# ScalarE as a further way for the weights' top halves into their bank and for the exponents' shift, in a new order of the work

## The chip, the cores and the metric

The kernel runs on one core of a Trainium2 chip. The metric is the device time of one execution in microseconds (us). A core has a matrix engine (TensorE, PE in the profile; PEld is its loading of the stationary operand), three engines for elementwise work (VectorE or DVE, ScalarE or ACT, GpSimd or POOL), and a queue that issues its transfers (SyncE or SP). Each engine works through its own list of instructions in order and waits where an operand is not there yet.

## What is computed

Attention over the 32 largest scores of each row, then two dense blocks over the 2304 tokens that come out of it:

```python
# q, k, v: 4 batches x 8 heads x 576 tokens x 64
scores = (q @ k.T) / 8
kth    = 32nd largest of each row
attn   = softmax(where(scores >= kth, scores, -1e9))
x = (attn @ v) rearranged to 2304 tokens x 512
h = x @ w_in                                   # 512 x 2048
x = (h * sigmoid(1.702 * h)) @ w_out           # 2048 x 512
a, b = x @ w1, x @ w2                          # 512 x 1024 each
out = (a * b @ w3) @ w4                        # 1024 x 1024, 1024 x 512
```

All inputs are float32. The kernel keeps more than one half-width number's precision by splitting each operand of a product into a high and a low float16 part and taking three products (high times high, low times high, high times low).

## The kernel before

The 2304 tokens are 18 tiles of 128 rows, and each tile has 8 heads, so there are 144 heads in order. For one head (`head`), TensorE makes the scores `S` (L1119, 128 x 576, in a bank pair `s_ps`), VectorE finds the 32 largest of each row by four rounds of eight (`max` L1139, with `match_replace` L1142 between them), and ScalarE makes the cut (L1157: entries under the 32nd largest are pushed far away; this frees the score bank) and the exp (L1160). The exp reads its shift, called `nb`, from one column: (32nd largest minus largest) times the head's scale. It is made by one one-column instruction (L1149) on GpSimd or on VectorE. The exp's result is split into a high part (L1172, or L1226 on GpSimd) and a low part (L1175, L1178), turned by a DMA (L1181), and multiplied with V on TensorE (L1195, L1197). When a tile has all its heads, `moe` runs the two dense blocks for it, whose products are the 512-column matmuls of L769 to L771.

The weights come in during the first 200 us, in 72 blocks of 128 x 512 (`load64`). They are stored as 64-bit words, so a block arrives as 512 KB (L487, on SyncE's queue), and four steps make a float32 of it: its upper bits are copied as a float16 ("top", L499 on ScalarE, L502 on GpSimd or L505 on VectorE); these are put into a PSUM bank ("pass", `f_pass`, L508: a matmul with the identity); VectorE shifts the lower word and ORs it with the bank ("join", L513), which frees the raw block's buffer for the next load. Six raw buffers and two more pairs hold arriving blocks. After the join come the weights' scaling and their split (`l2_scale`, with the squares on TensorE in L551; `split`: L599 or L605 high part, L608/L611 on TensorE or L621 on ScalarE, or L627/L624/L628 on GpSimd for the rest), the transposes of w3 (L680, L683) and the product of w3 and w4 (L806).

The work's order is not the order of the code. Every step is an `op` with one or more alternatives (engine, cost, function). A table `PLAN` holds a rank and the number of the chosen alternative for each step; `Order.run` sorts the steps by rank and issues them, each on the engine chosen, taking buffers from the pools in that order. What an engine does next is therefore fixed in the table, and a step that is late holds up everything behind it on its engine. The names in the profile are those of memory areas: `wout`, `win`, `w` and `usb` are stores that several kinds of data pass through, so `wout<-w` in L499 may be a block of any weight.

Of the kernel before, what the change touches and what calls it, by code (L numbers as in the profile page):

```python
# [37 lines left out]
class Order:  # L38
# [120 lines left out]
    'Tx+Yf)7ooYweH$LZLl^{yP^HndTFz?x!MwKmv%rqs2$QyYEQJMnxO-|f?h+ft=H3=>n-$_dON+dzF$9}U(}(2b!?2%=4t!23)&oQq4rSobU!^^K#zdM+A8gr'
    'hV-S{IxR?#(sSws0y+dZy3}*&dG!0*BdwTTU9YP*3TPI1O?#jX*Qe`;wNu&-{kZ-}e;m*=aG!ojzplT~JL!G&5Bg`_Gtvac27c6k=xL42Mt^;jp4&(?iW$j?'  # L160
    'jS|C*Tt*F}p|Mimq7OGF7>kV~fky+U==1f>#ulT8F~~S;+%z5-4+EouYwEQEQuVg_25qx;M!Tf#)h_yLx~^x^{R4va?0P;UDX^MR%V?!{)Til7^jZ3xfTj9!'
    '{i8<ow0e5Isoqr|pbyfQ>8teB`eyx(epi2>KhuBdzx7OpztLNtr(f2u=-c$2`YwI1eo{Xba6!MVS2x-kV~r_BPraW$SRbMf)ko-)^_luyeWAWvKh*GG!_y5{'
    'BwS6nmT)s+t-d~CUBZTh1qo*p4kw&T=wfs?dKrC<0mcYpv@zb8XiPQc8uJp@C2maoXXNr_@D=b)H)b}P(P%-VO~$swt%-XR^BM(>!bTCJs8P}=Ym_s}8+DBe'
    'M*YN&iTxAn8SNW2Xw;!mYonC!MPQ1rj?pqPHL+{r5@V^c%vf%$GIkjIj6=p5<FcX5Kr_OOH18*7Gz~Me`6w}yFTF3DFO6Bmm(EwxM-1EW8KFicqjF$Pqlxid'
    '|EIe~Izt%&fq_PdabJI_ztMl{aYnq6$0%XE)8FfVb#Cl24jRXe6GmsFPvA6Tj#0&^8raHcXN)u^8>@}A#$n@>amBc93^axsD~vV91><7iGvl*S+h}TxF=iQ8'
    'joZd2!!&OhcZ}!8E915C&iG<{HGUX>{~r?Fv`k<^Q<|<BVEW7uGt|s$#+$Xwie^J|t~oz-Uh0C>>}FM8PG1XOp`_wTm6EC_)k$ib+9q{yYGE@eH956r>S}Xc'
    '(%PgANnOlg=0tOnS=$_t+9Y*gYE)7QGtMky)-Zef>ihcm5|hfC70hbp5Ob_=q;IjWvf0^J&)418${gdH<6GrxpETUp)i=UNOxyHKKXbS7Eii`}YdWUCub`P='
    'zBkgEdCYv~G;^!D&D?LcHjnx)nm5fV=2UaKxyw9lUNxVXFU@o2H#5BzY*|(&E5r)5u9@$BepUtxT3M_}E6OTl^|A(8L#<*~D{HJZ&RT74ur^tntpnB}>x%Wj'
    'YGkIGjm>6ebF;rW${cS_HfNX{%}q%GL0N->f)*v6_nq?H@jXv^;d|@*?ptFXPdbuxE9s~C+x%<(GfgY4mCnj&`K)j&+R9^<Y@FD*RO13x#h`?sN<lfT;z7BB'
    '$_5p+QiJLRH4VyV<+lo2MXd5xW2?E<*6L_=wz^vVtzp&(Yn0W;8g31-##r;MMa32uTT*PfwX)cXVrz=svF=*;t%uet>z(!4`f2^P{#gV_;0Jsl9ApNSL2XbU'  # L170
    '<OX>`MNkFg1bIMFkN|XGf%G5%#DG{(5MVQl8E%#Y$sh$Z2W>%j&;twx<G?uMn(@*2X>cD1DjZZUsJc~JucJ5Co9J!yF#%%(o(EL3rdrdjh1M=>NbvaJ3BhMU'
    'IWvb9Yb9AFti3@ef=&h%hb3SQSQCzfsUgim+J<z8&){dMA%Zwc6Ph+OHnc131_!~(a0;9eGACq3$XS>jRYWyWEmQ~94sB7gL&;CjhYF%Xs5B}SRywRqSVKGt'
    'twUST4zwrqeCXAZk4pBy>+w#!4`0Eb!hVPS35y|(a9=zH&%m?8=7cQ>+Yla0^U>n81f4@WMs$kkAF+TEJI2ms7qH7kmW-?v*)B2<ZAaVF`Sc528nHfNL&ROm'
    '?RdMh-POKs_lz76IWO|FEm$gR&W1&8iMkQ>HtHW6Wv{Zg+S~0zk-H+#M_!8D%WrZ+xFVxS8yy&3E_%1f$J_DYd;~woM`mvp-63X^*e8yPW8%2D6n!W9LG&-N'
# [1391 lines left out]
```

## Time and profile before

| | us |
|---|---|
| median of 3 runs | 959.38 (959.14 to 960.53) |
| the profiled execution's own time | 956.57 |
| its span, first to last instruction | 954.8 |
| TensorE busy | 929.9 (97%) |
| VectorE busy | 870.4 (91%) |
| GpSimd busy | 781.8 (82%) |
| ScalarE busy | 676.4 (71%) |

The time lies 1.8 us above the span in the profiled execution, and that execution lies 2.8 us under the median. The program has three parts: in the first 50 us the weights and the first queries and keys arrive, and no engine is full; to 206 us heads 4 to 24 and the weights' work share all engines; from there on the weights are done and heads and dense blocks alternate. Matmuls overlap in TensorE's pipeline, so the recorded length of one (0.38 us) is longer than the distance to the next (0.216 us for 512 columns); the busy times of the table are unions and count the overlap once.

### The profile page before, as it was taken

The page shows a single profiled execution, that of the slowest core. Times are in us where ns is not written, and L with a number is a line of the kernel's source. Part 1 is how long each engine was busy: PE and PEld are TensorE (multiplying, and loading weights), DVE is VectorE, ACT ScalarE, POOL GpSimd, SP SyncE. Part 2 cuts the span into 40 slices and gives each one's busy share as a digit, 9 for nine tenths or more (in the row PEclk, how much of TensorE's full clock was granted, in tenths as well). Part 3 has the DMA queues.
Part 4 walks back from the last instruction along what each step waited for, and adds up shares of the span by engine and source line. Part 5 has one row for each costly group of instructions (what it writes and reads, how often), then busy time and mean ns, then how long its engine had stood idle before and what let it go on. Part 6 is the DMA issues. An engine that isn't in the chain of part 4 may idle for free.

```text
span 954.8 us, 19723 instructions
## 1 busy us (share of the span) xinstructions
PE 929.9 (97%) x6685; PEld 489.0 (51%) x6688; DVE 870.4 (91%) x1870; ACT 676.4 (71%) x1221; POOL 781.8 (82%) x1071
## 2 busy tenths in 40 slices
...
GB/s 302 309 293 324 283 256 204 204 121 128 161 155 145 163 154 130 146 127 154 147 162 115 171 122 139 146 150 156 128 132 131 117 123 138 127 83 116 55 3 34
DMA packets 397861, 149.30 MB, mean 156 GB/s; under 512 B 375872, under 2 KB 384064, under 8 KB 397760
## 3 DMA queue, kind: packets, MB, share of 16 engines
...
## 4 chain that ended last, share of the span: by engine, by line
PE 88%; DMA 5%; DVE 2%; POOL 1%; issue 1%; SPq 1%; ACT 1%; DVEq 0%; POOLq 0%; ACTq 0%
PE mm L769 23%; PE mm L770 22%; PE mm L771 22%; PE s_ps L1119 7%; PE mm L1197 4%; PE mm L806 3%; PE mm L1195 2%; DMA w<-in_moe_w_in_dram 1%; PE mm L551 1%; DMA w<-in_moe_w_dram 1%; DMA usb<-usb 1%; PE mm L611 1%; DVE ysb L1142 1%; DMA ats<-ysb 1%; PE mm L508 1%
## 5 line engine op out<-in xcount | busy, mean ns | idle before, releaser
L1139 DVE MAX8 m8s<-ysb 128x8 f32<-128x576 f32 x432 | 321.9, 755 | 6.1
L1142 DVE MATCH_REPLACE8 ysb<-m8s,ysb 128x576 f32<-128x576 f32 x288 | 214.0, 744 | 0.0
L1178 POOL TENSOR_TENSOR ysb<-ysb 128x512 f16<-128x512 f32 x144 | 167.9, 1169 | 0.3
L1157 ACT ACTIVATE ysb<-s_ps,m8s 128x576 f32<-128x576 f32 x144 | 106.5, 739 | 68.2 <-DVE m8s L1139 57.0
L1160 ACT ACTIVATE ysb<-ysb,nbs,small 128x576 f32<-128x576 f32 x144 | 123.9, 864 | 8.3 <-POOL nbs L1149 5.7
L771 PEld LDWEIGHTS <-usb 128*128 128x128 f16 x804 | 78.6, 98 | 95.0
L769 PE MATMUL mm<-w,usb 128*128 128x512 f16 x329 | 124.8, 379 | 2.2 <-DMA usb<-usb 1.6
L771 PE MATMUL mm<-w,usb 128*128 128x512 f16 x329 | 124.7, 379 | 0.0
L770 PE MATMUL mm<-w,usb 128*128 128x512 f16 x329 | 124.7, 379 | 0.0
L769 PEld LDWEIGHTS <-usb 128*128 128x128 f16 x804 | 78.5, 98 | 85.8 <-issue 2.7
L770 PEld LDWEIGHTS <-usb 128*128 128x128 f16 x804 | 78.6, 98 | 80.1 <-issue 0.9
L1139 DVE MAX8 m8s<-s_ps 128x8 f32<-128x576 f32 x144 | 108.7, 755 | 2.6 <-PE s_ps L1119 1.7
L1142 DVE MATCH_REPLACE8 ysb<-m8s,s_ps 128x576 f32<-128x576 f32 x144 | 107.9, 749 | 0.0
L1119 PE MATMUL s_ps<-kts,qts 128*128 128x288 f16 (+1 forms) x640 | 95.9, 290 | 1.3 <-ACT ysb L1157 1.3
L769 PE MATMUL mm<-wout,usb 128*128 128x512 f16 x239 | 90.6, 379 | 0.0
L771 PE MATMUL mm<-wout,usb 128*128 128x512 f16 x239 | 90.6, 379 | 0.0
L770 PE MATMUL mm<-wout,usb 128*128 128x512 f16 x239 | 90.6, 379 | 0.0
L769 PE MATMUL mm<-win,usb 128*128 128x512 f16 x236 | 89.4, 379 | 0.0
L771 PE MATMUL mm<-win,usb 128*128 128x512 f16 x236 | 89.4, 379 | 0.0
L770 PE MATMUL mm<-win,usb 128*128 128x512 f16 x236 | 89.4, 379 | 0.0
L1317 POOL TENSOR_TENSOR usb<-usb 128x512 f16<-128x512 f32 x59 | 68.4, 1161 | 16.1 <-issue 7.8
L1119 PEld LDWEIGHTS <-qts 128*128 128x128 f16 (+1 forms) x640 | 55.8, 101 | 41.0 <-issue 10.2
...
## 6 DMA issues: line engine op xcount, KB each, us to landing
...
```

What stands on the lines that cost most here:

```text
L769: nc.tensor.matmul(o, a[:, i, :], hi, start=(first and i == 0), stop=False)
L770: nc.tensor.matmul(o, a[:, i, :], lo, start=False, stop=False)
L771: nc.tensor.matmul(o, a[:, 4 + i, :], hi, start=False, stop=(last and i == 3))
L806: nc.tensor.matmul(E["mm"], e["f"][:, n * P : (n + 1) * P], E4[4 * kc + n]["w"], start=kc == 0 and n == 0, stop=kc == 1 and n == 3,)
L1119: nc.tensor.matmul(E["sp"][r : r + n, i], qe[q_][:, h, r : r + n], kt[:, j * S + i * HS : j * S + (i + 1) * HS], start=k_ == 0, stop=k_ == 1,)
L1139: nc.vector.max(out=E["m8"][:, 8 * i : 8 * i + 8], in_=E["sp"] if i == 0 else E["w"])
L1142: nc.vector.match_replace(out=two(E["w"]) if i == 0 else E["w"], in_to_replace=E["m8"][:, 8 * i : 8 * i + 8], in_values=E["sp"] if i == 0 ...
L1157: nc.scalar.activation(two(E["y"]), E["sp"], AF.Prelu, bias=E["m8"][:, TOPK - 1 : TOPK], scale=-1.0, alpha=1.0 / FAR)
L1160: nc.scalar.activation(E["y"], E["y"], AF.Exp, bias=E["nb"], scale=nesc)
L1178: return lambda: eng.tensor_tensor(hl()[:, S + SR : 2 * S], *y_of(at_main, SM), op=ALU.subtract)
L1197: nc.tensor.matmul(o[:, 0 : D + 1], at_, v2[:, j_, blk, D : P + 1], start=i == 0, stop=i == 8)
L1317: return lambda: eng.tensor_tensor(E["h"][:, C : 2 * C], src(), E["h"][:, 0:C], op=ALU.subtract)
```

## The change

It does three things.

1. `load64` gets a second way for the pass: a ScalarE copy of the top halves into the PSUM bank, beside the matmul with the identity.
2. `head` gets a third way for the shift: a pair of one-column ScalarE instructions. The first gives the 32nd largest minus the largest (Prelu with slope 1, scale -1 and a column as bias), the second multiplies it with the head's scale.
3. `PLAN` is another table: other ranks, and other alternatives chosen, among the old ones too.

```diff
+        def f_pass_a():
+            nc.scalar.copy(E["mm"], E["w"].bitcast(BF16)[:, 0:C])
+
...
-        ps_ = pe(0.22, due, f_pass, deps=[tp], env=E, acq=["mm"], tag="w pass")
+        ps_ = op([("T", 0.22, f_pass, 0.0), ("A", 0.5, f_pass_a, 0.0)], due, deps=[tp], env=E, acq=["mm"], tag="w pass")
...
+        def f_nb_a():
+            nc.scalar.activation(E["nb"], E["m8"][:, 0:1], AF.Prelu, bias=E["m8"][:, TOPK - 1 : TOPK], scale=-1.0, alpha=1.0)
+            nc.scalar.activation(E["nb"], E["nb"], AF.Copy, scale=esc)
+
...
-            [("G", 0.35, f_nb(nc.gpsimd), 0.0), ("V", 0.178, f_nb(nc.vector), NB_DVE)], due - 6, deps=[d, X["esc", hp]],
+            [("G", 0.35, f_nb(nc.gpsimd), 0.0), ("V", 0.178, f_nb(nc.vector), NB_DVE), ("A", 0.22, f_nb_a, 0.0)], due - 6, deps=[d, X["esc", hp]],
...
 PLAN = (
-    'c-jru1A87z00rRHaA#&`c2g_K7bi`cq;`_pO=`EPZQHhO+qP}nwt4S=IOja?(KJIdHK-BI)jTbW=BFiSNm`<2X+Xmo)3_$J^jZcjn--}B_=jtOnoo<?Vzgxc'
...
+    'c-jq@17jUa07h3cv!mUa-J18tO`4?Xt=%SRn<i~kyGd=^wr$(CZQHiZ_x{6&a}-5YG(}ga;wYJwoQj{Pgc7ZkRG@+sQ^5*TEKdec7LUIY;0abjl`y4{Qc6iw'
```

In the changed program the pass is a matmul for 25 of the 72 blocks and a ScalarE copy for 47 (at L511; lines after it stand 3 further down, and those after the new shift 7). The shift is on ScalarE for 94 heads (L1159 and L1160 there), on GpSimd for 36 instead of 101, and on VectorE for 14 instead of 43 (a tile that lies across two batches has more than one instruction). ScalarE has 12 fewer scalings of weights (32 to 27 of L599, 12 to 5 of L621) and 18 fewer high parts of the exp (110 to 92), GpSimd 18 more of these. The number of transfers is the same.

The first place is TensorE between the scores of head 5 and the next ones, where w3 and w4 are multiplied. Before, three passes stand there:

```order
L1119 MATMUL s_ps_89<-kts,qts 128x288
L508 LDWEIGHTS ident
L508 MATMUL mm_91<-wout,ident 128x512
L806 MATMUL mm_93<-w_70,usb 128x512 x2
L508 LDWEIGHTS ident
L508 MATMUL mm_91<-wout,ident 128x512
L806 MATMUL mm_93<-w_71,usb 128x512 x2
```

After, none (L809 is the old L806, L994 the sum for a key's scale, L570 that of a weight's scale):

```order
L1122 MATMUL s_ps_89<-kts,qts 128x288
L809 MATMUL mm_91<-w_70,usb 128x512
L809 MATMUL mm_91<-w_71,usb 128x512 x2
L809 MATMUL mm_91<-w_70,usb 128x512
L994 LDWEIGHTS ones
L994 MATMUL mm_93<-kvc,ones 128x1
L570 LDWEIGHTS ones
L570 MATMUL mm_92<-small,ones 128x1
```

The passes have left this list, and the products of w3 and w4 stand next to each other.

The second place is ScalarE at about the same point of the program. Before, cut (L1157), exp (L1160), top halves (L499) and the copy of a turned w3 block (L683) alternate:

```order
L1157 ACTIVATE ysb<-s_ps_89,m8s 128x576
L499 CAST wout<-w_70 128x512
L683 COPY usb<-mm_93 128x512
L499 CAST w_71<-w_70 128x512
L499 CAST wout<-w_70 128x512
L1160 ACTIVATE ysb<-ysb,nbs,small 128x576
L1172 CAST ysb<-ysb 128x576
```

After, passes (L511) stand between them (L1164 is the cut, L686 the old L683, L1179 the high part, L827 the old L824):

```order
L1164 ACTIVATE ysb<-s_ps_88,m8s 128x576
L511 CAST mm_93<-wout 128x512
L686 COPY usb<-mm_92 128x512
L499 CAST wout<-w_70 128x512
L1179 CAST ysb<-ysb 128x576
L499 CAST wout<-w_70 128x512
L511 CAST mm_92<-wout 128x512
L827 ACTIVATE wout<-mm_91,small 128x512
L511 CAST mm_93<-wout 128x512
```

Each pass that left TensorE's list is one instruction more in this one, ahead of the next cut or exp.

The third place is the shift in the middle of the program. Before, it stands on GpSimd between the low parts of the exp (L1175, L1178):

```order
L1317 TENSOR_TENSOR usb<-usb 128x512
L1175 TENSOR_TENSOR ysb<-ysb 128x64
L1149 TENSOR_SCALAR nbs<-m8s,small 128x1
L1178 TENSOR_TENSOR ysb<-ysb 128x512
L1175 TENSOR_TENSOR ysb<-ysb 128x64
```

After, it stands on ScalarE as a pair in front of the exp (L1167), with work of the dense block (L1318, L1349) between it and the cut:

```order
L1164 ACTIVATE ysb<-s_ps_88,m8s 128x576
L1318 CAST usb<-usb 128x512
L1349 ACTIVATE usb<-mm_92,msm 128x512
L1159 ACTIVATE nbs<-m8s 128x1
L1160 ACTIVATE nbs<-nbs,small 128x1
L1167 ACTIVATE ysb<-ysb,nbs,small 128x576
```

The one instruction on GpSimd has become two on the engine that also runs the exp.

## Rows read from the trace of the kernel before

**Rows 1.** Busy time of each engine in three stretches of the program; first line the columns.

```profile
core 0: us, PE busy (x) PEld busy (x) DVE busy (x) ACT busy (x) POOL busy (x), PEclk, DMA share, GB/s
0.00:50.00 50.00, 34.13 (x189) 20.00 (x190) 37.62 (x84) 28.70 (x56) 24.10 (x41) 1.00 1.00 308
50.00:206.00 156.00, 150.81 (x1009) 83.16 (x1011) 151.00 (x356) 131.60 (x238) 140.22 (x194) 1.00 0.98 243
206.00:876.00 670.00, 670.00 (x5010) 348.13 (x5009) 655.02 (x1386) 492.45 (x888) 595.68 (x813) 1.00 0.76 138
```

**Rows 2.** Timeline of TensorE at head 24's scores and at the end: start us, length us, what.

```profile
202.36 0.65 PE L1119 MATMUL s_ps<-kts,qts 128*128 128x288 f16 x4
...
950.40 0.38 PE L770 MATMUL mm<-w,tsb 128*128 128x512 f16 x1
950.61 0.38 PE L771 MATMUL mm<-w,tsb 128*128 128x512 f16 x1
```

**Rows 3.** Waits of TensorE, 50 to 206 us: total us, times, longest.

```profile
PE mm L769 <- DMA usb<-usb: 1.6, 1, 1.6
```

**Rows 4.** Waits of VectorE, 0 to 206 us, same columns.

```profile
DVE small L1074 <- ACT usb L1063: 6.0, 1, 6.0
DVE wout L513 <- POOL nbs L1149: 0.9, 1, 0.9
DVE win L513 <- PE mm L508: 0.7, 2, 0.4
```

**Rows 5.** L508 by stretch (before 34, after 37 us): length ns, minimum/median/maximum, starts.

```profile
L508 PE MATMUL mm<-w,ident x11: 582/588/634, 9.5 to 27.5; 128*128 128x512 bf16 x11
L508 PE MATMUL mm<-wout,ident x26: 376/379/383, 37.2 to 180.1; 128*128 128x512 bf16 x26
```

**Rows 6.** Instructions by line on ScalarE (count | busy us, mean ns | idle before), one timeline row.

```profile
L683 ACT COPY usb<-mm 128x512 f32<-128x512 f32 x16 | 9.1, 581 | 3.1 <-PE mm L680 2.9
L1311 ACT CAST usb<-usb 128x512 f16<-128x512 f32 x58 | 35.5, 617 | 6.3 <-POOL usb L1354 4.6 <-DVE usb L1348 1.6
L499 ACT CAST wout<-w 128x512 f16<-128x512 bf16 x17 | 11.2, 661 | 5.9 <-DMA w<-in_moe_w_dram 5.9
L1004 ACT ACTIVATE kvinv<-mm 128x1 f32<-128x1 f32 x22 | 3.6, 166 | 0.4 <-DVE kvc L1000 0.4
L1342 ACT ACTIVATE usb<-mm,msm 128x512 f32<-128x512 f32 x67 | 46.2, 689 | 29.8 <-PE mm L771 27.8 <-POOL msm L1331 1.5
L599 ACT ACTIVATE wout<-w,small 128x512 f16<-128x512 f32 x6 | 4.2, 717 | 0.0
404.85 1.63 ACT L1160 ACTIVATE ysb<-ysb,nbs,small 128x576 f32<-128x576 f32 x2
```

**Rows 7.** The exp and GpSimd's shift, same columns.

```profile
L1160 ACT ACTIVATE ysb<-ysb,nbs,small 128x576 f32<-128x576 f32 x144 | 123.9, 864 | 8.3 <-POOL nbs L1149 5.7 <-DVE nbs L1149 1.7
L1149 POOL TENSOR_SCALAR nbs<-m8s,small 128x1 f32<-128x1 f32 x101 | 37.6, 373 | 4.6 <-DVE m8s L1139 3.0 <-DVE msm L1296 1.0 <-DMA usb<-usb 0.3
```

**Rows 8.** VectorE by line, same columns; L426 to L1007 of 0 to 206 us.

```profile
L1149 DVE TENSOR_SCALAR nbs<-m8s,small 128x1 f32<-128x1 f32 x43 | 11.2, 261 | 0.3
L426 DVE SCALAR_TENSOR_TENSOR ysb<-ysb,kvc 128x576 f16<-128x576 f32 x1 | 1.2, 1216 | 0.9 <-ACT ysb L416 0.9
L831 DVE SCALAR_TENSOR_TENSOR wout<-mm,small,wout 128x512 f16<-128x512 f32 x1 | 0.7, 744 | 0.0
L1007 DVE TENSOR_SCALAR kvinv<-mm 128x1 f32<-128x1 f32 x5 | 0.7, 142 | 0.0
```

**Rows 9.** Waits of SyncE's queue, 0 to 206 us: total us, times, longest.

```profile
SPq L487 <- DVE wout L513: 14.1, 13, 2.6
```

**Rows 10.** Waits of ScalarE, 50 to 206 us, same columns.

```profile
ACT ysb L1157 <- DVE m8s L1139: 3.0, 3, 2.0
ACT win L499 <- DMA w<-in_moe_w_dram: 2.9, 2, 1.9
ACT ysb L1157 <- DMA ats<-ysb: 2.1, 1, 2.1
```

More of the change, by code (lines that the diff above doesn't have):

```diff
@@ L159 @@
[L159 to L174, printed above, removed]
@@ new lines @@
+    'Lm8k9Rz@jfm08L><*H(;{gp||TxE;0RoS8JR*oxYm3zu7<-77%X`{APJF7j^-s)g=h&o1{psrNcsCU$7s;$0I2PqSk>&gvfvNBWoplE6~HOTwVyGq%tWKeUc'
+    'zZIzFR{hm-YMi&acc-#f2~%U$1Ii&KMQx(CQoDOkdygnbm8t4H^`vr2*{WVv@2gL}nqN<~mwH{jt#(oSs-ILt<636Fv3@tyk7_0@w>C<htQOQ#w5D1szaf4}'
+    'TC&zqOVh@x)70_WG;OA~)9;MmPxZIDQroBPQ7@|dwG-N7?TMc!Fs~ZnE#i$<iJD2x>CL5{P;Po|d7deM6z=tSz3N|8_~rETYBSWC-dWzc>R0ubiu`QNPYqP_'
+    'c*E68>Rs<E?`!pfdP{xmeWLDHkEzGKr_}!H0ClJLpn6n2sh;(oSMRAW)i>UEYGEy2OYlq7(zV7~6TcQ(d9|WiNljF1t98@{YD2Y=+D#o+c0{Aujpj6JS9W}('
@@ new lines @@
+    'MU56WYF~C-*-m9Am2IvrYt*sPibnogh!&;g*9vH5v>2^|R#B_0)h*XItzKHcw9L`@{qy+y{A+6U)9R#kOsl4~OskRBI_<mqM^!alqnfK_(fqVPEuR*o6-q0X'
+    '7M<3noT+!!vgm)bV!G6e>v^>DX+_iG(gtYbv`N}zZHhKqo1-n$)@diTL)vTYnD#}xT+UC2dOrPYxu0pj(tf8|(b@eo_=oySE!eMwUrB9|wo%*Uw^=K#mD8$f'
+    ')wQ?k2k#dz(}rmywfWj&t(n@wJKwud?V<Jb8{{`iJFFem&iS3!DrxPs_F5+`yOv9f)QW4pwBFiqzv<d3?V@(c?~Zm=yQV$R9%|dQ9ojCxgIYJOyEa#wr#;o4'
+    'YcKs?X;-wH+AZz2c2~QnJ=0!jZ?t#Xd+mevP5bx%oaj2xGwPXij~<}s)eA&d^)KyT&3}Hh9kAFxLqLh>hW@esjr`~6d!koGABYauBhq`N_f3z|E9!;x%6epU'
@@ new lines @@
+    'dH+iON&cmx2m6=vAMZaw-=MG8H|sT`)6!d|4@|GAch`I9WAyg=A^(~FNBwK*?fg6VclB?ocTOLkJ|aC?Z|q;&zomb$9^+rszk+|9UPZ63x7H0kr+-O3TK}%8'
+    'x}&>#m|j+|t~b#e=p+5N>D%=k`WgL!{}X+!e%Sw#ep#QPAJ=c{xAjl@FaK;tgptw6VuTuz#y$Oo{!OO_F)|rZMvPI%=x+2dCKxr0ZpJ`kuCd=ZU>poMXB;uE'
+    '1l$U^ZFJN-={@z{`Y3&}K1H9d&(l}vEA^AnFZI{@d;ONK1>E(A0ju?6{yY6o`EQBdntm|-O1f^C1~!;s8JUe-hQ|mt@*4S!x<<#C5iz4;!i`b^MFV03d`8WH'
+    '0s*xG@*DL6N(3|rsAg0*8X9Rvy3x#NWehTg7^97`#zJGYvDjE+EH$>oY>3$!v(wnycu(U?jmH^NV<yH-i+N_eHr^QTj1R^~<BRdl_-*_(I0yofpe!f{%7aRv'
@@ new lines @@
+    'Ca48+f!rV%<OP8s1QZ5E00J3-KL`NfAOe&E>$Pp#N38}(0i8h)&>M^a<G@s~1pLs5o<sNQA-WTgJs@X5Ib(^sRNbO(Q+IiHd-r+Id3zdtjK0PSW22EhutZ>&'
+    'z^<U4-d3NaPt~XC0|M>@+zluQ%fp7S5o{ck7SuGTWzcAN8$N>&A;eJT;DW)$g9pLEa0;9XX9q0{S{bxD=s3)SB9IT2MrBdW;5rrBROpBnpijs)bD9-G;zE)_'
+    'W}3CoRCF3$K{wIW;5!xWRyctwn^nxZ<|uPX$hDB$A?0vObH2IETx%XTPlVhHxgV09gpzO)Lu!R~3GEs>HgpzIsh1X|#c3<rCTwun+^|^Ef^;Jj$!xMFbYtkA'
+    '&=*9f{b+wWkzS!w!={Dp4$I2&uwtwo8_kyIU6J=l-s@}t9Z6r)zmzeMw|3qEdH=C7d@7&CSMsQc(h;p9W?8>kMqZk?;2XpHg-;9r9Ddw7Wu3JyS+A_y5qBeA'
@@ new lines @@
+    'M-aP(-Oe6j&#)InZjIa*c{5V6Rok&c?3l>V$b69nB1_rZ?PK;y`-ZLNdlC5|@?&HHrJ7P$iB-xg6_q5Vs*<L(Ra%y5uXI#8DZQ1oYH6i{Qdw!FG*Ox<t(ES|'
+    '5am&s*UH;6KNLk>uWnQit38!{%5Y`0GDexLEL7GgYn469;WEb*p-R<Nzo|=<gUV^;jB-J_tUOR&DF2i<N`AF~T2QT_*3xQgowbX~L*<(CQTe9)Qm~pu4N(iL'
+    'QEG9uOxX%*V|AiNRZGpT2CJcJq*_u<P%EpcWm~H2)E(*(b&0l0+oP3G2dT+wRkgm_M;)jRS4XPL)#+tdsaMpS>Lc}r)>`eS4pm316V(OkYIU=EKs{9Uy^6~@'
+    'S~l&I_F4O@VV&w(^=x`>y`Wy$Ki)slzrVgvpQSI+kLcH<FX~TqWVl9Q<Gg-ff3CmM-$nn6Rt$fmyzxx`pnuVS=zsLmMp>hs(aZ2NLX46|MI$jLIi|MJ+n8=N'
```

156 lines of the change are left out of this document (76 added, 80 removed).

## The prediction

> **What bounds the kernel now.** I read the busy time by stretches first, then the waits of TensorE and VectorE, then the last matmuls. From 206 us to 876 us TensorE is busy 670.00 of 670.00 us [rows 1], and its waits have no line there or later. The kernel ends with it: the last 512-column matmuls start 0.21 to 0.22 us apart, the last at 950.61 us [rows 2], and only one output copy and its store follow. So the end is set by when TensorE gets past its last wait, plus work that does not change: from the scores of head 24 (202.36 us) [rows 2] to the end both programs hold the same matmuls. The change can only act on the time at which those scores come up.
>
> Up to there two engines are full. From 50 to 206 us VectorE is busy 151.00 of 156 us, TensorE 150.81, ScalarE 131.60, GpSimd 140.22 [rows 1]. TensorE's waits there are few, the longest 1.6 us for a turned tile that a DMA brings [rows 3]. VectorE carries each head's maxima and the join of each weight block, and it was busy 37.62 + 151.00 = 188.6 of the first 206 us. The other 17.4 us are waits, one of 6.0 us for the first query tile and small ones [rows 4]. I take both engines as near-bound before head 24, and VectorE as the one that the change hardly relieves.
>
> **The passes.** 47 of the 72 weight blocks no longer cross TensorE, all of them before head 24: 12 before head 4, 35 between heads 4 and 24, for which I take the stretch from 50 to 206 us. At the spacing of [rows 2] that is 47 x 0.216 = 10.2 us, less one L608 matmul more and a few others: 9.9 us off TensorE's work, all before its gapless stretch. The recorded 0.38 us of a pass [rows 5] holds the pipeline's depth and isn't its price.
>
> On ScalarE each is a new copy, SBUF to PSUM, 512 wide. No row shows one. The nearest are the copy out of PSUM, 581 ns, the cast inside SBUF, 617, and the cast from the raw block, 661 [rows 6]. Consecutive ScalarE instructions overlap: two exps that take 864 ns each [rows 7] lie in 1.63 us [rows 6], 0.1 less than their sum. So 0.48 to 0.56 us a pass; I take 0.50, nearest to the copy. 35 x 0.48 to 0.56 = 16.8 to 19.6 us land in the stretch 50 to 206.
>
> **The shift.** 94 heads take ScalarE's pair of one-column instructions, 16 of them by head 24, 13 between heads 4 and 24. A one-column copy takes 166 ns [rows 6]; a scale read from a column adds about 689 - 581 = 108 [rows 6]. Each half of the pair has one such operand. So 2 x (0.166 - 0.1) = 0.13 us if all overlaps, 2 x (0.166 + 0.108) = 0.55 if nothing does; I take 0.35. 13 x 0.13 to 0.55 = 1.7 to 7.2 us. What it replaces: 0.373 us on GpSimd (65 fewer in all) and 0.261 on VectorE (29 fewer) [rows 7, 8]. The exp waits 5.7 us for GpSimd's shift and 1.7 for VectorE's over the whole kernel [rows 7], but an exp is not what TensorE waits for after 206, so 0 us of that counts.
>
> By the Trainium skill (ScalarE: Activation LUTs, section What ACT_TABLE_LOAD costs) each column operand adds about 93 ns to an activation of 186 + 0.833 N ns, and neighbours overlap by about 93. The row agrees on the operand (108) and on the overlap (0.1); as an estimate from that page a pair is 0.47 us, 13 pairs 6.1, near my upper end.
>
> **The rest of the new order, up to head 24.** ScalarE loses 12 scalings of weights (L599, L621) at 0.717 us [rows 6] less 0.1 each, so 7.4, to GpSimd, and gains 3 top halves at 0.56, so 1.7. Between heads 4 and 24 its load becomes 131.6 + (16.8 to 19.6) + (1.7 to 7.2) - 5.7 = **144.4 to 152.7 of 156 us**. VectorE loses 7 shifts (7 x 0.261 = 1.8) and one split of a K tile (1.2), and five single moves of 0.14 to 0.74 us come to +0.1 [rows 8]: **2.9 us less**. GpSimd takes over what ScalarE sheds and gives up 10 shifts, some us more in all on its 140.22, which has room. Queued behind the passes on ScalarE are cuts and exps, whose cut frees the scores' bank for TensorE; behind the join, on VectorE, the maxima; behind a late join, on SyncE's queue, the next weight load, which already waited 14.1 us for joins into one pool alone [rows 9]. No DMA is added or moved to another queue.
>
> **The sum.** TensorE alone would come 9.9 us earlier. VectorE's work up to the same scores falls by 2.9 only, and with its 17.4 us of waiting unchanged head 24 comes 2.9 us earlier; TensorE then waits for the other 7. Some of VectorE's waiting may go with the passes and GpSimd's shifts: three waits on L508 (0.7, 0.7, 0.6) and 0.9 on a GpSimd shift [rows 4], together 2.9. I don't count them, since the joins now wait for ScalarE instead. Against the profiled execution: 956.57 - 2.9 = 953.7. That execution is 2.8 below the median of 959.38; against the median it is **956.5**, at best 959.4 - 5.8 = 953.6. After head 24 the 78 remaining pairs add 10 to 43 us (at 0.13 to 0.55) to a ScalarE that is busy 492.45 of 670 [rows 1], which waits more than that; this costs 0.
>
> **Rivals.**
> *TensorE alone sets head 24*, and gets the whole 9.9: 949.5. For it: it is as busy as VectorE. Against it: VectorE would have to lose 7 us of its 17.4 us of waits, of which 6.0 are the one at the start. Chance 0.06.
>
> *ScalarE becomes the bound between 50 and 206 us.* The middle of its load is 148.5. It waits there 3.0 us for maxima, and 2.9 and 2.1 for transfers in the longest lines, with smaller transfer waits of 1.7 and 1.5 about 11 us in all [rows 10], which the change doesn't remove. With all of them kept it needs 148.5 + 11.2 = 159.7 us, 3.7 more than the stretch has: 963.1. It decides from an added load of 156 - 131.6 - 11.2 = 13.2 us, if no wait shrinks; if half of them shrink, since work is then queued over them, from 18.8. It would show as waits of VectorE's joins and of TensorE's scores on ScalarE. Chance 0.24, and this is the slower side.
>
> *Nothing is left of it.* The joins' waits on ScalarE eat the 2.9: that takes 2.9 / 35 = 0.08 us a pass, where the waits on TensorE's passes were 2.0 us for 72, 0.03 each. A ScalarE instruction in front lasts 0.6, a matmul in front 0.2, so 0.08 is in reach. 957.5 to 961.3, say 959. Chance 0.24.
>
> *A later rise of TensorE's clock.* Passes before 34 us last 588 ns, those from 37 us on 379 [rows 5]: the first are at the lower level (1.2 GHz), though the granted clock of 0 to 50 us reads 1.00 [rows 1]. With 12 early passes gone TensorE does less there. If the rise came 10 us later, the 10 x 34.13 / 50 = 6.8 us of work in them would take twice as long, and at most 6.8 us would be lost: 966.2, less the 2.9: 963.3. Before 50 us TensorE idles 15.9 us [rows 1], which speaks against it. Chance 0.04.
>
> The Trainium skill (TensorE: Matmul & The Clock Gate, Part 1) has it that the throttled clock is the default and that activity releases it. By that rule fewer early matmuls could delay the rise, and this rival's time would hold; the rows agree on slow early passes and show nothing of what would delay the rise.
>
> **Chances and range.** The forecast, with its own range of 953.6 to 957.4, has 0.42. A measurement of this kernel tells about 0.2% (1.9 us) from no change. Faster than that: 0.42 + 0.06 = 0.48; within it 0.24; slower 0.24 + 0.04 = 0.28. The range reaches down past the best case by 1.6 and up to just over the ScalarE rival's and the clock rival's times: 952.0 to 963.5; the full gain below it and a ScalarE at its upper end (152.7 + 11.2 = 163.9, so 967) stay out.
>
> **What would show it.** Right: TensorE's stretch without waits begins 2 to 4 us earlier, some 7 us more idle time on TensorE before it, on scores or grams that follow VectorE; VectorE at 97% or more of 50 to 206; ScalarE at 144 to 153 there; a pass at 0.58 to 0.66 us by itself. Wrong: joins (L516) waiting for ScalarE by more than 3 us in all, scores waiting for cuts, or ScalarE without gaps from 50 to 206 (the ScalarE rival); head 24 earlier by over 7 us (the TensorE rival); early matmuls long after 37 us (the clock rival); waits of TensorE after 210 us, on exps or turned tiles, would break the first step, that nothing after head 24 matters.

## The result, and the profile after

| | us | ratio to the kernel before | 95% interval |
|---|---|---|---|
| kernel before, 4 runs | 959.83 (959.14 to 960.53) | | |
| changed kernel, 4 runs beside it | 950.60 (949.35 to 951.64) | 0.9903 | 0.9886 to 0.9920 |
| kernel before, 21 runs | 958.12 (956.29 to 960.69) | | |
| changed kernel once more, 5 runs beside it | 951.65 (950.77 to 952.44) | 0.9928 | 0.9915 to 0.9942 |

The change makes the kernel faster, by 7 to 9 us; the larger set of runs says 6.9. The forecast was 956.5, its range ended at 952.0, and both medians lie under that. Effects below are (ratio - 1) x 958.5 us; by this scale the changed kernel stands at -6.9.

The page of the kernel after, busy time by engine (share of the span, instructions):

```profile
PE 921.8 (97%) x6641; PEld 484.6 (51%) x6642; DVE 865.2 (91%) x1838; ACT 724.5 (76%) x1426; POOL 785.2 (83%) x1045
```

TensorE lost 8.1 us of 929.9 and kept its share of 97%; ScalarE's busy time rose by 48 us from 676.4. The stretches, in the columns of [rows 1], with the end of the second at the cut of head 23:

```profile
0.00:50.00 50.00, 32.12 (x186) 20.31 (x187) 38.68 (x90) 36.28 (x77) 32.38 (x52) 0.97 0.97 311
50.00:199.50 149.50, 144.56 (x969) 78.22 (x968) 145.42 (x340) 145.04 (x283) 139.10 (x187) 1.00 1.01 254
206.00:876.00 670.00, 670.00 (x5011) 348.33 (x5010) 648.71 (x1350) 517.82 (x1020) 596.23 (x788) 1.00 0.76 138
```

Where before ScalarE had room between 50 us and head 24 (131.60 of 156 [rows 1], 84%), it is now as full as TensorE and VectorE: of 149.5 us TensorE is busy 144.56, VectorE 145.42, ScalarE 145.04 (97% each), GpSimd 139.10 (93%). After 206 us TensorE is again busy all the time. Timeline of TensorE, as in [rows 2], at the scores of head 24 and at the end:

```profile
195.89 0.65 PE L1122 MATMUL s_ps<-kts,qts 128*128 128x288 f16 x4
...
944.22 0.38 PE L774 MATMUL mm<-w,tsb 128*128 128x512 f16 x1
```

Head 24's scores came 6.47 us earlier than in [rows 2], the last matmul 6.39 us earlier. Nearly all of the difference is there at head 24; behind it under 0.1 us is lost.

Waits of VectorE, 0 to 206 us, to set beside [rows 4] (L516 is the join, L511 ScalarE's pass, L508 TensorE's):

```profile
DVE small L1077 <- ACT usb L1066: 5.8, 1, 5.8
DVE w L516 <- ACT mm L511: 3.0, 2, 2.2
DVE w L516 <- PE mm L508: 0.7, 2, 0.4
```

The joins that waited 2.0 us for TensorE's passes now wait 3.0 us for ScalarE's and 0.7 for TensorE's. The new instructions of ScalarE (columns of [rows 6]), and one pair of the shift in the timeline:

```profile
L511 ACT CAST mm<-wout 128x512 f32<-128x512 bf16 x21 | 12.2, 586 | 0.4 <-DVE wout L516 0.2
L1159 ACT ACTIVATE nbs<-m8s 128x1 f32<-128x1 f32 x94 | 27.4, 292 | 4.5 <-DVE m8s L1142 4.5
L1160 ACT ACTIVATE nbs<-nbs,small 128x1 f32<-128x1 f32 x94 | 27.7, 295 | 4.0
314.25 0.29 ACT L1159 ACTIVATE nbs<-m8s 128x1 f32<-128x1 f32 x1
314.57 0.29 ACT L1160 ACTIVATE nbs<-nbs,small 128x1 f32<-128x1 f32 x1
314.77 0.61 ACT L1352 ACTIVATE usb<-usb 128x512 f32<-128x512 f32 x1
```

A pass takes 586 ns, and by the starts in the trace the next instruction begins 0.52 us after it (median of 47). In the pair the second half begins 0.32 us after the first, which it reads, and the next instruction 0.20 us after the second: 0.52 us a pair.

### The profile page after: what moved, and what is told of

It reads as the page before. It is cut to its first block, busy times and chain, and to the rows that moved or that the text cites. A ratio compares the mean times of both kernels' runs of the same rounds, so it can differ in the third digit from the quotient of the medians.

```text
span 948.4 us, 19725 instructions
## 1 busy us (share of the span) xinstructions
PE 921.8 (97%) x6641; PEld 484.6 (51%) x6642; DVE 865.2 (91%) x1838; ACT 724.5 (76%) x1426; POOL 785.2 (83%) x1045
## 4 chain that ended last, share of the span: by engine, by line
PE 82%; ACT 5%; POOL 4%; DVE 3%; DMA 3%; issue 2%; SPq 1%; ACTq 0%; POOLq 0%; DVEq 0%
PE mm L772 23%; PE mm L774 22%; PE mm L773 22%; PE s_ps L1122 7%; PE mm L1204 4%; PE mm L1202 2%; DMA w<-in_moe_w_out_dram 1%; DVE ysb L1145 1%; DVE m8s L1142 1%; ACT mm L511 1%; DMA tsb<-in_moe_w_dram 1%; DMA ysb<-in_k_dram 1%; ACT ysb L1167 1%; PE mm L614 1%; POOL wout L631 1%
## 5 line engine op out<-in xcount | busy, mean ns | idle before, releaser
L1185 POOL TENSOR_TENSOR ysb<-ysb 128x512 f16<-128x512 f32 x142 | 164.3, 1160 | 0.3
L1164 ACT ACTIVATE ysb<-s_ps,m8s 128x576 f32<-128x576 f32 x144 | 106.2, 738 | 56.4 <-DVE m8s L1142 45.6
L772 PE MATMUL mm<-w,usb 128*128 128x512 f16 x377 | 142.9, 379 | 0.0
L774 PE MATMUL mm<-w,usb 128*128 128x512 f16 x377 | 142.9, 379 | 0.0
L773 PE MATMUL mm<-w,usb 128*128 128x512 f16 x377 | 142.9, 379 | 0.0
L774 PEld LDWEIGHTS <-usb 128*128 128x128 f16 x824 | 80.6, 98 | 97.2
L1167 ACT ACTIVATE ysb<-ysb,nbs,small 128x576 f32<-128x576 f32 x144 | 123.7, 865 | 5.2 <-POOL nbs L1152 2.3
L772 PEld LDWEIGHTS <-usb 128*128 128x128 f16 x824 | 80.5, 98 | 86.4 <-issue 2.6
L773 PEld LDWEIGHTS <-usb 128*128 128x128 f16 x824 | 80.6, 98 | 82.6
L772 PE MATMUL mm<-win,usb 128*128 128x512 f16 x240 | 91.0, 379 | 0.0
L774 PE MATMUL mm<-win,usb 128*128 128x512 f16 x240 | 90.9, 379 | 0.0
L773 PE MATMUL mm<-win,usb 128*128 128x512 f16 x240 | 90.9, 379 | 0.0
L774 PE MATMUL mm<-wout,usb 128*128 128x512 f16 x207 | 78.5, 379 | 0.0
L773 PE MATMUL mm<-wout,usb 128*128 128x512 f16 x207 | 78.4, 379 | 0.0
L772 PE MATMUL mm<-wout,usb 128*128 128x512 f16 x207 | 78.4, 379 | 0.0
L1204 PEld LDWEIGHTS <-ats 128*128 128x128 f16 (+1 forms) x1440 | 68.4, 100 | 9.3 <-issue 4.3
```

The lines of the kernel that those rows point to most:

```text
L772: nc.tensor.matmul(o, a[:, i, :], hi, start=(first and i == 0), stop=False)
L773: nc.tensor.matmul(o, a[:, i, :], lo, start=False, stop=False)
L774: nc.tensor.matmul(o, a[:, 4 + i, :], hi, start=False, stop=(last and i == 3))
L1164: nc.scalar.activation(two(E["y"]), E["sp"], AF.Prelu, bias=E["m8"][:, TOPK - 1 : TOPK], scale=-1.0, alpha=1.0 / FAR)
L1167: nc.scalar.activation(E["y"], E["y"], AF.Exp, bias=E["nb"], scale=nesc)
L1185: return lambda: eng.tensor_tensor(hl()[:, S + SR : 2 * S], *y_of(at_main, SM), op=ALU.subtract)
```

## The experiments

Theories, as they stand in the expectations. V: VectorE sets head 24 (the forecast's). T: TensorE does, so its 9.9 us count in full. O: the new order made the gain. B: TensorE and VectorE hold each other in turn. E: the new order fills all engines, so each is held by the others. F: something with a fixed place in the old order holds it, loads above all.

### Undoing the two moves, and making one of them alone

Passes back on TensorE, in the new order:

```diff
-        ps_ = op([("T", 0.22, f_pass, 0.0), ("A", 0.5, f_pass_a, 0.0)], due, ...
+        ps_ = op([("T", 0.22, f_pass, 0.0), ("T", 0.22, f_pass, 0.0)], due, ...
```

> The changed kernel with its 47 passes on TensorE again, everything else (order, shifts, other choices) as it is. TensorE's list grows by 47 x 0.216 = 10.2 us before head 24. Theory T (TensorE's early work counts in full, whatever VectorE does): the time goes back up by 8 to 10 us, to 959 to 961, and TensorE's scores of head 24 come 7 to 10 us later. Theory V (VectorE sets head 24, the forecast's theory; the gain came from its 2.9 us less of work and from its shorter waits): the time rises by 2 to 3 us only, to 953. Theory O (the new order made the gain, not the passes): no change, 950 to 952.

Measured: 965.75, ratio 1.0082 (1.0069 to 1.0094): 14.8 us slower than the changed kernel, more than the 10.2 us of work that came back, and slower than the kernel before. VectorE's waits up to 220 us:

```profile
DVE w L516 <- PE mm L508: 7.0, 6, 2.8
DVE wout L516 <- PE mm L508: 3.0, 3, 1.2
DVE win L516 <- PE mm L508: 2.2, 2, 1.9
```

Joins wait 12.2 us for passes. VectorE idles 31.0 us up to head 23's last maximum, against 15.4. V with its constant waits falls in the new order, and O falls too: without the passes on ScalarE the new order is worse than the old one.

Shifts back, to GpSimd, passes left on ScalarE:

```diff
-            [("G", 0.35, ...), ("V", 0.178, ...), ("A", 0.22, f_nb_a, 0.0)], due - 6, ...
+            [("G", 0.35, ...), ("V", 0.178, ...), ("G", 0.35, f_nb(nc.gpsimd), 0.0)], due - 6, ...
```

> The changed kernel with the 94 shifts that ScalarE makes put on GpSimd (one instruction of 0.37 us each, 35 us more on GpSimd in all, 16 x 0.37 = 6 us by head 24), passes and order as they are. Theories T and O: within 1 us of the changed kernel (950 to 952), since no exp is what TensorE waits for. Theory V: the same or up to 1 us slower. If the move of the shift carries the gain, by shorter waits of the exps, the time rises by 4 us or more.

Measured: 973.09, 1.0154 (1.0140 to 1.0167): 21.7 us slower than the changed kernel. Only 5.6 of these are there at head 24 (its scores come at 201.5 us); 18 come later. The exp on ScalarE, and TensorE's waits from 206 to 876 us, which the changed kernel does not have:

```profile
L1167 ACT ACTIVATE ysb<-ysb,nbs,small 128x576 f32<-128x576 f32 x144 | 123.8, 866 | 44.1 <-POOL nbs L1152 42.0 <-DVE nbs L1152 0.6
...
PE s_ps L1122 <- ACT ysb L1164: 2.8, 6, 1.2
PE mm L772 <- ACT usb L1358: 2.3, 3, 1.5
```

The exps wait 42.0 us in all for GpSimd's shift, where it was 5.7 in the old order [rows 7], and TensorE is busy 657.84 of these 670 us. The waits shown are for cuts (L1164) and for a step of the dense block (L1358), which stand in the same list of ScalarE as the late exps. So exps that are late can reach TensorE; in the kernel before they did not. GpSimd is also busier here (612.86 us against 596.23), and this run does not part the two.

Both undone:

> The changed kernel with both moves undone: passes on TensorE, shifts on GpSimd; what is left of the change is the new order and the other choices. Theory T: 959 to 962, no gain left. Theory V: 953 to 954, since VectorE keeps its 2.9 us. Theory O: 950 to 952.

Measured: 984.41, 1.0270 (1.0255 to 1.0284). The order, with its other choices and without the two moves, is 26 us worse than the old one. O is out.

The same 47 passes on ScalarE in the old order, each at the place of its matmul:

```diff
-        ps_ = pe(0.22, due, f_pass, deps=[tp], ...
+        if n in ON_ACT:
+            ps_ = act(0.5, due, f_pass_a, deps=[tp], ...
+        else:
+            ps_ = pe(0.22, due, f_pass, deps=[tp], ...
```

> The kernel before, old order and all old choices, with the same 47 blocks' passes made by ScalarE at the place in the order where TensorE made them; shifts as before. Theory T: the gain comes without the new order, 950 to 952, unless ScalarE, to which nobody made room in the old order, holds the joins up. Theory V: 956 to 958. Theory O: 959 or slower, the joins waiting for a ScalarE that is queued with other work.

Measured: 963.25, 1.0054 (1.0040 to 1.0067), 5.2 us slower than before. VectorE's waits there, 0 to 220 us (L520 is the join, L515 ScalarE's pass):

```profile
DVE wout L520 <- ACT mm L515: 5.3, 6, 1.9
DVE w L520 <- ACT mm L515: 3.9, 4, 2.2
DVE win L520 <- ACT mm L515: 2.2, 2, 1.3
```

The joins wait 11.4 us for passes that stand behind other work in ScalarE's old list. The move does not carry the gain without an order that has it in its places. T, too, would have seen a gain here but for these waits, so T needed the next group.

### Ten microseconds on or off one engine, old order

Each of these adds or takes some 10 us of work on one engine before head 24 (one run takes it on two, one on the loads) and changes nothing else. Of TensorE's 47 extra passes 12 stand before head 4, where it idles in any case, so 35 x 0.216 = 7.6 us of them fall in the full stretch.

```diff
# TensorE more: the pass of the 47 blocks twice          # VectorE more: the join of 15 blocks twice
+            for _ in range(2 if n in ON_ACT else 1):     +            for _ in range(2 if n in TWICE else 1):
                 nc.tensor.matmul(E["mm"], ...                            nc.vector.scalar_tensor_tensor(E["w"]...
# TensorE less: 12 products of w3 and w4 left out        # VectorE less: no third match_replace in 12 heads
+            if n == 1 and (kc == 0 or f >= 4):           +            if i == 2 and 5 <= 8 * t + h < 17:
+                continue                                 +                return
# ScalarE more: the top halves of 18 blocks twice        # loads less: 12 loads move half their bytes
+            for _ in range(2 if n in TWICE else 1):      +            k = 2 * C if n in HALF else 4 * C
                 nc.scalar.copy(top(), first())                           nc.sync.dma_start(raw()...[:, 0 : k - 1], ...
```

> The kernel before, with TensorE's matmul of the pass issued twice for the 47 blocks that the change takes off it: 47 x 0.216 = 10.2 us more on TensorE before head 24, nothing else. Theory T (TensorE's early work counts in full): 10 us slower, 968 to 969. Theory V (VectorE sets head 24): TensorE has 5 to 6 us of waits between 50 and 206 us to put it in, so 3 to 5 us slower, 961 to 963. A theory that both count, each step of one waiting for the other in turn (theory B): 5 to 9 us slower.

> The kernel before, with the join issued twice for 15 blocks between heads 3 and 22: 15 x 0.68 = 10.2 us more on VectorE, nothing else. Theory T: VectorE waits little between 50 and 206 us (5 us), so most of it must show even so, 5 us or more, unless TensorE had work to go on with. Theory V: 10 us slower in full, 968 to 969. Theory B: 5 to 9 us.

> The kernel before, with 12 of the 64 products that make w3 times w4 left out, two float32 matmuls of 0.43 us each: 12 x 0.86 = 10.3 us less on TensorE between heads 4 and 20, in the old order, and on no other engine anything changed (so part of the product is not computed). Theory T: 9 to 10 us faster, 948 to 950. Theory V: 2 us faster at most, 956 to 958. Theory B: 4 to 7 us faster.

> The kernel before, without the third match_replace of heads 5 to 16 (their last eight maxima are then found again among the same values, so the selection of these heads is not the right one): 12 x 0.83 = 10 us less on VectorE between heads 5 and 16, nothing else. Theory T: no change, 957 to 959. Theory V: 9 to 10 us faster, 948 to 950. Theory B: 2 to 6 us faster.

> The kernel before with both cuts at once: 12 of the 64 products of w3 and w4 left out (10.3 us less on TensorE) and the third match_replace of heads 5 to 16 left out (10 us less on VectorE), so part of the product and the right selection of those heads are missing. By themselves they brought 1.5 and 2.1 us. Theory B (in the old order the two engines wait for each other in turn, so that each alone is held by the other): clearly more than the sum, 7 to 10 us faster, 949 to 952. Theory F (the old order is held by something else, ScalarE, GpSimd, or loads, whose places in the order are fixed): about the sum, 3 to 4 us, 955 to 956.

> The kernel before with ScalarE's copy of the top halves issued twice for 18 blocks between heads 4 and 24: 18 x 0.56 = 10.1 us more on ScalarE, which is busy 131.6 of 156 us there. Theory E (the old order left ScalarE room, and the change's gain is that this room is used): under 3 us slower, 958 to 961. Theory F: 5 to 10 us slower, since what stands in its order is late whether it has room or not.

> The kernel before with 12 of the weight loads between the 20th and the 56th moving half their bytes (the other half of these blocks is what stood in the buffer before, so these weights are wrong): 12 x 256 KB = 3.1 MB less, some 10 us of the transfers of 50 to 125 us at the 300 GB/s that they reach there. Theory F (loads hold the old order, at a transfer share of 1.0 up to 150 us): 5 us faster or more. If TensorE's chain of 100 to 150 us holds it, as the chain of waits says: under 2 us.

| old order | ratio | 95% interval | us |
|---|---|---|---|
| TensorE +10.2 | 1.0014 | 1.0004 to 1.0024 | +1.3 |
| VectorE +10.2 | 1.0067 | 1.0055 to 1.0079 | +6.4 |
| ScalarE +10.1 | 1.0017 | 1.0006 to 1.0028 | +1.6 |
| TensorE -10.3 | 0.9984 | 0.9975 to 0.9992 | -1.5 |
| VectorE -10 | 0.9973 | 0.9957 to 0.9990 | -2.6 |
| TensorE -10.3 and VectorE -10 | 0.9959 | 0.9945 to 0.9973 | -3.9 |
| loads -3.1 MB | 0.9988 | 0.9977 to 1.0000 | -1.2 |

T falls: 10 us off TensorE, at no cost anywhere, bring 1.5. V falls by half: VectorE's extra work shows in great part, but taking 10 us off it brings only 2.6. B falls: both at once give 3.9, about the sum of the two (4.1), not more. F as loads falls: 1.2, where 5 or more were expected of it. The chain of waits, shares by line from 100 to 150 us, shows why. A second profiled execution of the kernel before (the first has the same lines in front, L806 with 34.4%):

```profile
by line: PE mm L806 37.0%; PE mm L611 17.4%; PE mm L551 14.7%; PE mm L508 8.8%; PE s_ps L1119 5.9%; PE mm L612 4.3%; PE mm L1197 3.2%; PE mm L608 2.7%; PE mm L1195 1.8%; PE mm L680 1.8%; PE mm L769 0.9%; PE mm L770 0.9%; PE mm L771 0.9%; PE
```

The same stretch with TensorE and VectorE relieved:

```profile
by line: DMA ats<-ysb 24.9%; PE mm L611 7.6%; PE mm L551 7.3%; POOL ysb L1182 6.7%; POOL wout L502 3.9%; PE mm L808 3.4%; PE mm L508 3.4%; POOL w L842 3.3%; issue 3.2%; ACT win L599 2.7%; ACT w L499 2.4%; POOL wout L624 2.4%; POOL wout L628
```

In the old order the whole stretch is TensorE's own list (L508's passes 8.8% of it), one product after the other with no wait between. That chain speaks for theory T. With TensorE and VectorE relieved it is gone, and turned tiles, GpSimd's low parts, weights' splits and ScalarE have taken its place, and the time falls by 3.9 us only. So the chain of one execution does not say what its engine is worth: 37% of it is L806, and 10.3 us off that line brought 1.5. Several chains of nearly one length beside each other would give this, a list that is relieved at one place waiting at the next for one that is not; no run shows these chains singly. GpSimd, busy 140.22 of 156 us [rows 1], was not loaded or relieved by itself, in this order or the new one.

### Ten microseconds on or off one engine, new order

The same edits on the changed kernel; ScalarE's is the pass of 20 blocks issued twice, TensorE's extra work 12 products of w3 and w4 issued twice.

> The changed kernel without 12 of the 64 products of w3 and w4 (part of the product is missing): 10.3 us less on TensorE before head 24. Theory T: 9 to 10 us faster than the changed kernel's 951.6, 942. Theory E (the new order fills all engines, each is held by the other three): 1 to 3 us faster, 949 to 951.

> The changed kernel with 12 of the products of w3 and w4 issued twice (the product is not the right one): 10.3 us more on TensorE before head 24, on no other engine anything. It takes back what the passes gave TensorE, without taking the copies from ScalarE. Theory T and theory E: 7 to 10 us slower, 959 to 961. Theory V, with TensorE's 5 us of waits from 50 us on to put it in: 3 to 5 us slower, 955.

> The changed kernel with the join issued twice for 15 blocks: 10.2 us more on VectorE before head 24 (in the old order the same cost 6.3 us). VectorE waits 4 us in the stretch from 50 us to head 24. Theory V: 6 to 10 us slower. Theory T: under 3 us. A theory that in the new order all engines are equally full there (theory E: GpSimd, ScalarE, VectorE and TensorE at 93% or more, so what any of them gains is given to all): 6 to 10 us.

> The changed kernel with ScalarE's pass issued twice for 20 blocks between heads 4 and 24: 20 x 0.49 = 9.8 us more on ScalarE, which is busy 145 of 149.5 us there. Theory E: 6 to 10 us slower. Theory V, and theory T: ScalarE's extra work is hidden, under 3 us slower.

| new order | ratio | 95% interval | us, against -6.9 |
|---|---|---|---|
| TensorE -10.3 | 0.9927 | 0.9913 to 0.9942 | -0.1 |
| TensorE +10.3 | 1.0007 | 0.9998 to 1.0016 | +7.6 |
| VectorE +10.2 | 1.0020 | 1.0011 to 1.0029 | +8.8 |
| ScalarE +9.8 | 1.0044 | 1.0031 to 1.0056 | +11.1 |

Here 10 us more on any of the three costs three quarters of it or more, and 10 less on TensorE bring nothing that the interval shows. A theory of one engine has no place for all three; theory E has, though it expected 1 to 3 us of the last. The busy time from 50 to 206 us (columns of [rows 1]), with TensorE's extra work:

```profile
50.00:206.00 156.00, 152.18 (x990) 82.26 (x989) 145.12 (x338) 144.75 (x280) 137.56 (x185) 1.00 0.98 241
```

With VectorE's:

```profile
50.00:206.00 156.00, 142.91 (x942) 76.49 (x941) 150.52 (x346) 143.59 (x277) 136.25 (x183) 1.00 1.00 242
```

With ScalarE's:

```profile
50.00:206.00 156.00, 140.35 (x921) 75.20 (x920) 140.99 (x326) 150.43 (x291) 133.59 (x178) 1.00 0.97 241
```

In each the engine with the extra work is the busiest (152.18, 150.52, 150.43 of 156), and the others fall behind it. The chain of the changed kernel, second profiled execution, 100 to 150 us:

```profile
by line: DMA tsb<-in_moe_w_dram 15.7%; DMA ysb<-in_k_dram 11.3%; DVE ysb L1145 9.4%; issue 6.8%; ACT ysb L1167 6.3%; DVE m8s L1142 5.3%; POOL ysb L1185 4.5%; PE mm L614 3.9%; ACT ysb L1164 3.9%; DVE wout L516 2.6%; ACT win L499 2.5%; SPq L4
```

Loads, maxima, exps, low parts and products alternate, and TensorE has 3.2 of the 50 us (its pieces there, added up).

### The same kernels again, and the early passes

> The kernel before once more, for a second profiled execution. The executions of it so far spread from 955 to 961 us, the profiled one (956.57) near the lower end. Theory K (the spread is the clock of TensorE in the first 50 us): early passes longer, or the change from about 588 to 379 ns a pass later than 35 us, in a slower execution. Theory L (it is the landing of the weight loads): the clock's change at the same time, and waits on loads longer by the difference.

Measured: 959.11, 1.0007 (0.9995 to 1.0018). The second profile's span is 957.0 us, against 954.8. At the scores of head 8 the second is 2.0 us behind, and 2.0 to 2.2 from there to the end, so what differs between these two is made early. The first 50 us of the second (columns of [rows 1]):

```profile
0.00:50.00 50.00, 30.97 (x178) 18.20 (x179) 34.95 (x75) 27.44 (x54) 22.17 (x39) 0.90 0.99 301
```

The granted clock is 0.90 where it was 1.00 [rows 1]. Closer, from 33 to 38 and from 41 to 44 us:

```profile
33.00:38.00 5.00, 2.59 (x22) 1.93 (x22) 4.85 (x9) 2.40 (x4) 4.21 (x7) 1.00 1.07 319
41.00:44.00 3.00, 3.00 (x13) 1.91 (x12) 2.05 (x4) 1.65 (x3) 2.83 (x4) 0.55 1.05 397
```

TensorE had been busy 2.59 of 5 us and 1.98 of the next 3, and then the clock stood at 0.55 for three microseconds, near the lower of its two levels (1.2 and 2.4 GHz), while TensorE was busy throughout. In the first profile these stretches read 1.00. The larger part of the missing 0.10 lies elsewhere: from 23.00 to 30.20 us the clock reads 0.53 here and 1.00 in the first profile, whose passes took 588 ns there all the same [rows 5]. So a reading of 1.00 that early did not mean the upper level. By a pass at about the same time, in the first profile and in the second, the slower execution even came to the upper level sooner:

```profile
30.50 0.63 PE L508 MATMUL mm<-wout,ident 128*128 128x512 bf16 x1
30.92 0.38 PE L508 MATMUL mm<-wout,ident 128*128 128x512 bf16 x1
```

Theory K falls as it stands, passes that are slow for longer. What the clock did was to rise and fall again, and the second execution was 0.8 us behind before that fall (scores of head 2) and 2.6 behind it (head 4), so the fall can have made up to 1.8 us. L is not excluded, and these are two executions, no more. Over all 103 executions of the kernel before that were timed beside the experiments, the mean granted clock (0.990 to 1.000) and the time hardly go together (correlation -0.19), so the clock as recorded does not explain their spread from 955 to 961 us.

> The changed kernel once more, for its size against more runs and a second profile: 950.6 by the runs so far, 949 to 952; 0.991 of the time before. The second profile shows scores of head 24 near 196 us again, and TensorE without waits from there.

Measured: as in the first table. The second profile has head 24's scores at 197.9 us and a span of 950.5; against the second profile of the kernel before (204.6, 957.0) that is 6.6 and 6.5 us.

The 12 passes ahead of head 4 on TensorE again, the other 35 on ScalarE:

```diff
+        other = ("T", 0.22, f_pass, 0.0) if n in EARLY else ("A", 0.5, f_pass_a, 0.0)
-        ps_ = op([("T", 0.22, f_pass, 0.0), ("A", 0.5, f_pass_a, 0.0)], due, ...
+        ps_ = op([("T", 0.22, f_pass, 0.0), other], due, ...
```

> The changed kernel with the 12 passes ahead of head 4 on TensorE again and the other 35 on ScalarE. It gives TensorE 12 matmuls in the stretch in which its matmuls still run at half pace. If their absence delays the clock's rise (the clock rival; in the changed kernel a pass still took 577 ns at 35 us, in the kernel before 378 from 37 us), the rise comes back by 2 to 3 us and the time falls by 1 to 2 us, to 950. If the new order's early part needs the passes on ScalarE (theory E), it is 1 to 5 us slower, 953 to 957.

Measured: 950.49, 0.9921 (0.9903 to 0.9939), the same as the changed kernel within the intervals. The clock did differ in the profiles. The changed kernel from 33 to 36 and 36 to 39 us:

```profile
33.00:36.00 3.00, 1.33 (x9) 0.72 (x9) 3.00 (x9) 2.15 (x4) 2.92 (x5) 0.86 0.95 336
36.00:39.00 3.00, 3.00 (x23) 2.62 (x22) 2.97 (x7) 2.90 (x6) 2.92 (x3) 0.57 1.18 209
```

With the early passes on TensorE, 36 to 39 us:

```profile
36.00:39.00 3.00, 2.66 (x26) 1.91 (x25) 2.97 (x7) 2.32 (x4) 2.92 (x3) 1.00 1.08 241
```

Without the early passes the clock fell to 0.57 after a stretch in which TensorE was busy 1.33 of 3 us; with them it stayed at 1.00. The time is the same all the same. So the early passes give or cost nothing that these intervals show, the 35 between heads 4 and 24 carry what the passes carry, and no version here beats the changed kernel by more than a measurement tells.

## Why the prediction was wrong

**What bounds the kernel: right.** From the start of head 24's scores to the end of the span are 752.4 to 752.5 us in the kernels before and after, both profiles, and at most 753.4 in all others, but for the two with shifts put back on GpSimd (770.5 and 769.7). The step "an exp is not what TensorE waits for" holds only while ScalarE gets the shift in time; those two showed its limit.

**TensorE's work: nearly right.** 9.9 us were counted; up to head 24 its busy time fell by 8.2 in the first pair of profiles (181.3 to 173.1) and by 8.6 in the second (181.0 to 172.4). In the first pair the fall of the clock at 36 to 39 us, which the kernel before did not have there, accounts for about 1.3 of the missing 1.7 (an estimate from that row, 3.00 x 0.43). In the second pair both kernels have such a fall, and where the missing 1.3 are is open. What did not come is "TensorE then waits for the other 7": its idle time before head 24 grew by 1.8 and 1.9 us only.

**The clock rival: not seen.** It was a later rise. These are transposes of a weight block, first in the kernel before, then in the changed kernel, first profiles:

```profile
32.35 1.06 PE L680 MATMUL mm<-ident,w 128*128 128x128 f32 x4
32.08 0.60 PE L683 MATMUL mm<-ident,w 128*128 128x128 f32 x4
```

The changed kernel was at the upper level first; in the second profiles both were by 31 us. What it had was a fall after the rise, and the gain came in spite of it; with the early passes back the profile shows no such fall, and the time did not change.

**"With its 17.4 us of waiting unchanged": the step that failed.** VectorE up to head 23's last maximum (columns of [rows 1]): the kernel before and the changed kernel, first profiles, then the same two, second profiles:

```profile
0.00:204.12 204.12, 183.06 (x1166) 101.80 (x1170) 186.74 (x434) 158.81 (x289) 162.51 (x231) 1.00 0.99 261
0.00:197.49 197.49, 174.67 (x1148) 97.76 (x1149) 182.12 (x425) 179.31 (x355) 169.47 (x236) 0.99 1.00 269
0.00:206.23 206.23, 182.62 (x1169) 101.23 (x1170) 186.41 (x434) 159.19 (x289) 162.39 (x231) 0.98 0.98 258
0.00:199.52 199.52, 173.98 (x1149) 97.36 (x1149) 182.83 (x425) 179.54 (x354) 169.72 (x236) 0.99 1.01 267
```

VectorE's own work was sized nearly right: 2.9 us were counted, and its busy time fell by 4.6 and 3.6 (the summed lengths of its instructions by 3.6 and 2.7). Its waits were held constant, and they fell from 17.4 to 15.4 us and from 19.8 to 16.7, by 2.0 and 3.1. Work and waits together are the 6.6 and 6.7 us by which that maximum came earlier. The working had a sum with 2.9 us of waits in it, 5.8 us, as its best case, 953.6, and set the range's low end only 1.6 below that, at 952.0; it took 2.9 as the forecast on the ground that joins would wait for ScalarE instead. They did: the joins' waits for passes of either engine rose from 2.0 to 3.7 us, and from 2.8 to 4.0 in the second pair. But VectorE's other waits fell by more than that, and the sum had listed only one of them. These are waits of VectorE in the second profile of before, 0 to 206 us, that the changed kernel's second profile does not list at all; whether the order or the moved instructions took them away, no run tells:

```profile
DVE wout L513 <- POOL ysb L1175: 1.5, 1, 1.5
DVE w L513 <- ACT ysb L1157: 1.3, 1, 1.3
DVE mm L562 <- PE mm L551: 1.1, 1, 1.1
```

The passes' waits of the changed kernel, same view:

```profile
DVE w L516 <- ACT mm L511: 2.6, 4, 1.3
DVE w L516 <- PE mm L508: 1.1, 3, 0.6
```

**VectorE as the one engine that sets head 24: wrong for both orders.** The seven runs on the old order show no single one, with VectorE the nearest to it (6.4 of 10.2); the four on the new order show three that cost three quarters or more of what is put on them. A forecast from one engine's sum needed a second question: how much of each engine's idle time the new order can still use. The rows answered a part of it: ScalarE idle for 24.4 of 156 us, the other engines at 90% or more.

**ScalarE: sizes right, rival wrong.** Its load came out at 145.0 us up to head 23's cut, in the range worked out (144.4 to 152.7). A pass is 0.52 us (0.50 taken). The pair is 0.52, at the upper end of 0.13 to 0.55 and over the 0.35 taken: the second half reads the first's result, and the overlap that the low end assumed is not there between them. The rival's price rested on 11.2 us of waits that "the change doesn't remove"; ScalarE's idle time there went from 24.4 to 4.5 us. The waits shrank with other work queued over them, which the working named and then weighed too low.

**The rival nearest in its number**, TensorE's full 9.9 (949.5, chance 0.06), is not so in its mechanism: 10 us off TensorE at no cost bring 1.5 us in the old order and 0.1 in the new one, and head 24 came 6.5 and 6.6 us earlier, not the "over 7" that was to be its sign.

**What stays open.** How the 6.9 us divide between the passes, the shifts and the order. The passes alone in the old order and the order alone (both moves undone) are each slower than the kernel before; the shifts alone in the old order and a new order for the old choices were not run. The table's other choices (12 scalings and 18 high parts off ScalarE) were not undone by themselves either, and GpSimd, which takes them over, was not tested. Shown is only that the passes do not gain in an order that was not made for them, nor this order without either of the moves; that the gain is ScalarE's idle time put to use fits all runs and was not isolated.
